# Cluster masks of the later head pairs moved from TensorE to VectorE, with first-layer weight sums and loads moved in the order

## The chip, the core and the metric

The kernel runs on one core of a Trainium2 chip. The metric is device time in microseconds (us) of the whole launch; less is better. A timed run has no profiler attached; one further execution was recorded by the hardware profiler, and all views and durations below come from it.

## The reference

Routed attention followed by a two-layer network with a hard-swish gate, everything in float32:

```python
# q, k, v: (4, 8, 768, 64), centroids: (8, 16, 64), w_in: (512, 2048), w_out: (2048, 512)
q_assign = argmax(normalised(q) . normalised(centroids))     # one of 16 clusters for each query
k_assign = argmax(normalised(k) . normalised(centroids))     # and for each key
mask = q_assign[:, :, :, None] == k_assign[:, :, None, :]
scores = where(mask, q @ k^T / 8, -1e9)
attn = softmax(scores);  x = attn @ v                        # a query sees the keys of its own cluster
# x as (3072, 512) tokens
h = x @ w_in;  g = h * clip(h + 3, 0, 6) / 6;  out = g @ w_out
```

## The kernel before

Attention works on *pairs* of heads, `g` = 0 to 15 (four batches of four pairs). A pair has 12 *items* `n`: two halves of the queries (`hf`, 384 each) times six chunks of 128 keys (`j`). For one item, both heads at once (64 rows of the array each):

- `scores` (line 419) writes keys by queries into PSUM: one f32 part from `xf` (q and k turned by `turn`) and one bf16 part from `xm`. `xm` holds the one-hot cluster vectors, turned by `route_turn` (line 367); on the side of k they hold -2^60 in every cluster but the key's own. The sum of the two parts is the score where the clusters agree and about -2^60 where they don't, so the exponential is 0 there. That is the mask.
- `exponentials` (line 434, ScalarE) writes `ex`; there are six buffers of it.
- `key_sums` (lines 454 and 457, GpSimd) adds `ex` up over the chunks, into `acc`.
- `attn_v` (line 467, TensorE) adds `ex` times v into `pv`; after six chunks `divide` sums `acc` over partitions by TensorE (`pd`, line 488), takes the reciprocal on VectorE (492), and multiplies (493). The result goes to DRAM as `xd`.

Before a pair can start, it is loaded (`load`, line 195, six DMAs on SyncE's queue), turned (310), routed (`cluster_scores` 323, `route` 334 to 343: scores against the centroids, maximum, one-hot) and its one-hots are turned (367).

The network works on 12 *blocks* of 256 tokens. A block is 8 *up* items and 7 *down* items. Both layers use a scheme with fewer multiplications (Strassen's, in Winograd's form), so sums of weights are needed. For the first layer these are `tx` (T1, T2, T4 of one up item; line 570), made once, written to DRAM as `td` and loaded again for the later blocks (line 573), two items ahead, into three buffers; T3 overwrites a part of `w_in_sb`. The up items of block 0 use plain products (603). An up item of the later blocks (`halved`) writes two PSUM banks, `uX` and `uY` (line 648; one of each, in turn), which VectorE reads with six sums and copies (659, 666); then ScalarE lifts (516), VectorE clips (519), and after every second item GpSimd makes four sums (`gated_sums`, 638). A down item (683) is one 128x256x1024 product, with the sums of y on VectorE (690).

The order of all engines is written out by hand (`tc.manual_schedule()`): each engine runs its instructions in the order in which the loop below emits them. The loop over `n` takes two items at a time (a *step*; `r` is the step's place in the pair, 0, 2, ... 10). From `DECODED` (item 96, pair 8) on, `four_by_four` runs: steps with r = 2, 6 and 10 emit scores and exponentials, and then a *fill* of four or five network items, with the preparation of the next pair between them (turns at r = 2, routing at 6, one-hots at 10); steps with r = 0, 4 and 8 emit scores, exponentials, the division and `attn_v` of four items, and key sums. `later` and `checks` hold work for the step after (the store of `num`, range checks).

`MASKED` is the first pair whose masks VectorE makes; before, it is `NPAIR` (16), so that none are, and `by_vector`, `clusters`, `spread` and `masks` are never in effect.

Of the kernel before, what the change touches and what calls it, by code (L numbers as in the profile page):

```python
# [17 lines left out]
C = 16  # L18
# [98 lines left out]
def fast_path(ctx, tc, ok, q, k, v, centroids, moe_w_in, moe_w_out, out):  # L117
# [48 lines left out]
    counts = const.tile([P, 2, NPAIR], F32, name="counts")  # L166
    w_low = const.tile([P, 1], F32, name="w_low")

    MASKED = NPAIR
    st = {}  # L170
    later = []
    numbers = []
# [87 lines left out]
    cen = startp.tile([P, D], F32, name="cen")  # L260
    parity = const.tile([P, 2], F32, name="parity")

    number = const.tile([P, C], BF16, name="number")

    def constants():
        make_identity(nc, ident)
        for t in range(2):
            nc.vector.tensor_reduce(
                out=parity[:, t : t + 1],
                in_=ident.rearrange("p (h t c) -> p t h c", t=2, c=C)[:, t], axis=AX.XY, op=ALU.max,  # L270
            )
        nc.gpsimd.memset(half_c, 0.5)
        nc.gpsimd.memset(low_c, 1.0 / BOUND)
        nc.gpsimd.memset(ones, 1.0)
        nc.gpsimd.memset(w_low, W_LOW)
        nc.gpsimd.memset(one_hot, 0.0)
        for c in range(C):
            nc.gpsimd.memset(number[:, c : c + 1], float(c))

        warm = psum_t.tile([P, 4, P], F32, name="warm", tag="t")  # L280
        for i in range(14):
            nc.tensor.transpose(out=warm[:, i % 4], in_=ident, identity=ident)
# [47 lines left out]
    def route(g):  # L330
        cs = st.pop(("cs", g))
        pr = scratch([P, NC2, 2, C], "pr")
        for i in range(NC2 // 4):
            nc.tensor.transpose(out=pr[:, 4 * i : 4 * i + 4], in_=cs[:, i], identity=ident)
        pr = pr.rearrange("p j t c -> p (j t) c")
        mx = rtp.tile([P, 2 * NC2], F32, name="mx")
        nc.vector.reduce_max(out=mx, in_=pr, axis=AX.X)
        oh = one_hot.rearrange("p j (t c) -> p j t c", t=2)[:, :, :, 0:C]
        pr = pr.rearrange("p (j t) c -> p j t c", t=2)
        mx = mx.rearrange("p (j t) -> p j t", t=2)  # L340
        halves = [slice(0, NCH), slice(NCH, NC2)]
# [14 lines left out]

        later.append(count)
        if g >= MASKED:
            numbers.append(lambda: clusters(g))

    def route_turn(g, part):
        if part == 0:
# [11 lines left out]
        return where(n)[0] >= MASKED  # L374

    def clusters(g):
        oh = one_hot.rearrange("p j (t c) -> p j t c", t=2)[:, :, :, 0:C]
        which = rtp.tile([P, NC2, 2, C], BF16, name="which")
        nc.vector.tensor_tensor(
            out=which, in0=oh, in1=number.unsqueeze(1).unsqueeze(1).to_broadcast([P, NC2, 2, C]), op=ALU.mult  # L380
        )
        qid = st["qid"] = rtp.tile([P, NCH, 2], BF16, name="qid")
        kid = st["kid", g] = kidp.tile([P, NCH, 2], F32, name="kid")
        nc.vector.tensor_reduce(out=kid, in_=which[:, NCH:], axis=AX.X, op=ALU.add)

        nc.vector.tensor_scalar(
            out=kid, in0=kid, scalar1=-1.0, scalar2=C * (C - 1) / 2.0, op0=ALU.mult, op1=ALU.add
        )
        qsum = rtp.tile([P, NCH, 2], F32, name="qsum")
        nc.vector.tensor_reduce(out=qsum, in_=which[:, 0:NCH], axis=AX.X, op=ALU.add)  # L390
        nc.vector.tensor_copy(out=qid, in_=qsum)

    def spread(g, part):
        if part == 0:
# [13 lines left out]
        return (g, *divmod(r, NCH))  # L408

    def scores_qk(n):  # L410
        g, hf, j = where(n)
        st["ps", n] = psum_s.tile([P, 2, 512], F32, name="ps")
        scores_part(n, st["xf", g], True)

    def scores_part(n, x, first):
        g, hf, j = where(n)
        for t in range(2):
            r = slice(t * D, (t + 1) * D)
            nc.tensor.matmul(  # L419
                st["ps", n][:, t, 0:HALF], lhsT=x[r, NCH + j],  # L420
                rhs=x[r, hf * NHC : (hf + 1) * NHC], start=first,
                stop=not first or by_vector(n),
            )

    def scores(n):
        if ("ps", n) not in st:
            scores_qk(n)
        if not by_vector(n):
            scores_part(n, st["xm", where(n)[0]], False)

    def exponentials(n):
        sc = st.pop(("ps", n))[:, :, 0:HALF]
        ex = st["ex", n] = expp.tile([P, 2, HALF], F32, name="ex")
        nc.scalar.activation(out=ex, in_=sc, func=ACT.Exp, scale=SM_SCALE)  # L434

# [12 lines left out]

# [111 lines left out]
    def first_sums(u):  # L560

        blk, i = divmod(u, HF)
        if not 0 < blk < B * NHC:
            return
        tx = st["tx", u] = txp.tile([P, 3, HK, P], F32, name="tx")
        if blk == 1:
            t1, t2, t4 = (tx[:, k] for k in range(3))
            b11, b12, b21, b22 = wi(0, 0, i), wi(0, 1, i), wi(1, 0, i), wi(1, 1, i)
            for out_, in0, in1 in ((t1, b12, b11), (t2, b22, t1), (t4, b21, t2), (b12, b22, b12)):
                nc.vector.tensor_tensor(out=out_, in0=in0, in1=in1, op=ALU.subtract)  # L570
            nc.sync.dma_start(td[:, i], tx)
        else:
            nc.sync.dma_start(tx, td[:, i])

    def token_sums(b, m):

# [15 lines left out]
    def ffn_items(b):  # L592
        def up(m, i):
            def item():
                load_block()
                u = (b * NHC + m) * HF + i
                g = g_sb[:, 0:4, i]
                if u < HF:
                    ph = psum_m.tile([P, 512], F32, name="ph", tag="m")
                    for t in range(2):  # L600
                        f = t * HF + i
                        for kt in range(NKT):
                            nc.tensor.matmul(  # L603
                                ph[:, t * HC : (t + 1) * HC], lhsT=w_in_sb[:, kt, f * P : (f + 1) * P],
                                rhs=st["xb", b, m][:, kt], start=(kt == 0), stop=(kt == NKT - 1),
                            )
                    ph = ph.rearrange("p (k c) -> p k c", k=4)
                    lift(g, ph)
                    clip(g, g, ph)
                    gated_sums(i)  # L610
                else:
                    halved(b, m, u, i, g)
                if u >= HF or i < HF - 2:
                    first_sums(u + 2)
                if i == HF - 1:
                    st.pop(("xb", b, m)), st.pop(("xs", b, m), None)
                    st["free"] = True
                    load_block()
                    finish()

            return item
# [70 lines left out]
        def down(m, part):  # L692
            def item():
# [85 lines left out]

    st["early"] = st["free"] = True  # L780
    st["last"] = False
    fill, checks, unmasked = [], [], []
    st["done"], st["valued"] = 0, DECODED - lag_v

    def check_all():
# [8 lines left out]
    def four_by_four(n, r, steps):  # L794
        for i in steps:
            scores(i)
        if r % 4 == 2:
# [22 lines left out]
        for i in range(st["valued"], min(n, total)):  # L820
            attn_v(i)
            if i % per_pair == NCH - 1:
                later.append(divide(i))
        st["valued"] = min(n, total)
        for i in steps[1 if r == 8 else 2 :]:
            exponentials(i)
        for i in steps:
            masks(i)
            key_sums(i)

    with tc.manual_schedule():
# [18 lines left out]
        for n in range(0, total + lag_d + 2, 2):  # L850
# [436 lines left out]
```

## Time and profile before

| | us |
|---|---|
| median of three timed runs | 1033.52 (1029.15 to 1035.98) |
| the profiled execution | 1026.24 |
| its span, first to last instruction | 1024.4 |
| TensorE (PE) busy | 997.8 (97%) |
| VectorE (DVE) busy | 562.8 (55%) |
| ScalarE (ACT) busy | 390.0 (38%) |
| GpSimd (POOL) busy | 433.3 (42%) |
| granted TensorE clock | 0.997 of full speed |

The chain that ended last is followed back from the last instruction; its shares tell who holds up the end. Busy shares are means over stages that differ: until about 250 us the weights are decoded beside the attention and all engines are busy; from there to 797 us attention and network alternate; the rest is network alone. A busy TensorE is not one at its peak, and the ends of its rows are modelled, so starts are compared. In a row of the timeline the first number is the start in us from the start of the span, the second the length; what stands in brackets is the idle time of that engine just before, and what ended it. A row can merge several instructions (xN).

### The profile page before, as it was taken

What the parts mean: (1) busy time and instruction counts of PE and PEld (TensorE: products, weight loads), DVE (VectorE), ACT (ScalarE), POOL (GpSimd) and SP (SyncE); (2) the same over time, 40 slices, a digit from 0 to 9 for tenths busy, and PEclk for the clock granted to TensorE, in tenths of its full rate; (3) what the DMA queues carried; (4) which work ended last, traced back from release to release, by engine and by line L of the source; (5) the groups of instructions that cost most, each with busy time, mean ns of one, the idle gap of its engine ahead of it and who ended that gap; (6) DMA issues with size and microseconds to landing.
All of it is one profiled execution on the core that took longest, in us unless ns stands there. A gap on an engine that the chain in (4) does not pass through costs nothing.

```text
span 1024.4 us, 16727 instructions
## 1 busy us (share of the span) xinstructions
PE 997.8 (97%) x6560; PEld 738.4 (72%) x6560; DVE 562.8 (55%) x1085; ACT 390.0 (38%) x764; POOL 433.3 (42%) x363
## 2 busy tenths in 40 slices
PE   8999999999999999999999999999999999999996
PEld 4444445546778777778787777678787898999995
DVE  4899977868368245226336236227246272727270
ACT  6888876675233233233323333333223020202010
POOL 4777756766325426426415415524516230303030
PEclk9999999999999999999999999999999999999999
DMA  6355664532223222223224025023023051414120
GB/s 177 101 145 144 165 165 97 143 86 46 58 91 110 55 91 83 54 75 103 58 83 118 27 68 152 9 70 98 29 84 97 3 154 40 143 40 126 51 63 25
DMA packets 107176, 90.34 MB, mean 88 GB/s; under 512 B 78416, under 2 KB 88656, under 8 KB 107088
## 3 DMA queue, kind: packets, MB, share of 16 engines
q1 hardware_dynamic: 106944, 89.15, 31.1%
q8 instruction: 54, 0.88, 0.3%
q14 instruction: 34, 0.28, 0.1%
q10 hardware_dynamic: 144, 0.03, 0.0%
HBM read 73.43 MB, written 15.73 MB: 87 GB/s over the span
## 4 chain that ended last, share of the span: by engine, by line
PE 84%; ACT 4%; DVE 4%; DMA 4%; SPq 2%; issue 1%; POOL 0%; ACTq 0%; DVEq 0%; POOLq 0%
PE Y L683 16%; PE uY L648 14%; PE ps L419 12%; PE X L683 12%; PE uX L648 11%; PE pv L467 9%; PE ph L603 3%; SPq L195 2%; PE pd L488 2%; PE pqk L310 2%; DMA raw<-in_moe_w_in_dram 1%; ACT ex L434 1%; PE pcs L323 1%; DMA tx<-td 1%; DVE wunit L247 1%
## 5 line engine op out<-in xcount | busy, mean ns | idle before, releaser
L457 POOL TENSOR_TENSOR acc<-acc,ex 128x768 f32<-128x768 f32 x128 | 241.3, 1885 | 139.0 <-ACT ex L434 132.6
L638 POOL TENSOR_TENSOR g_sb<-g_sb 128x256 f32<-128x256 f32 x176 | 130.5, 763 | 325.9 <-DVE g_sb L519 322.5
L434 ACT ACTIVATE ex<-ps 128x768 f32<-128x768 f32 x192 | 148.4, 806 | 87.4 <-PE ps L419 75.3
L516 ACT ACTIVATE sx<-g_sb,half_c 128x512 f32<-128x512 f32 x88 | 63.5, 722 | 277.5 <-DVE g_sb L659 277.5
L419 PE MATMUL ps<-xf 64*128 64x384 f32 x768 | 165.5, 509 | 2.7 <-ACT ex L434 2.6
L467 PE MATMUL pv<-ex,vt 128*64 128x384 f32 x768 | 141.1, 496 | 0.0
L690 DVE TENSOR_TENSOR y<-y,Y 128x256 f32<-128x256 f32 x48 | 20.2, 421 | 175.5 <-PE Y L683 174.7
L467 PEld LDWEIGHTS pv<-ex,vt 128*64 128x64 f32 x768 | 48.7, 136 | 78.2 <-issue 70.0
L492 DVE RECIPROCAL rcp<-pd 128x384 f32<-128x384 f32 x32 | 81.8, 2556 | 41.4 <-PE pd L488 41.3
L419 PEld LDWEIGHTS ps<-xf 64*128 64x128 f32 x768 | 63.1, 186 | 53.1 <-issue 36.5
L454 POOL TENSOR_TENSOR acc<-ex 128x768 f32<-128x768 f32 x32 | 59.8, 1867 | 94.9 <-ACT ex L434 94.9
L648 PE MATMUL uX<-xb,w_in_sb 128*128 128x128 f32 x704 | 93.8, 277 | 0.0
L683 PE MATMUL X<-w_out_sb,g_sb 128*128 128x256 f32 x384 | 89.7, 381 | 0.0
L683 PE MATMUL Y<-T,g_sb 128*128 128x256 f32 x384 | 87.3, 380 | 0.0
L683 PE MATMUL Y<-w_out_sb,g_sb 128*128 128x256 f32 x384 | 87.2, 380 | 0.0
L648 PEld LDWEIGHTS uX<-xb,w_in_sb 128*128 128x128 f32 x704 | 86.5, 194 | 0.0
L683 PEld LDWEIGHTS X<-w_out_sb,g_sb 128*128 128x128 f32 x384 | 71.3, 190 | 12.6 <-issue 3.8
L683 PEld LDWEIGHTS Y<-T,g_sb 128*128 128x128 f32 x384 | 72.3, 190 | 11.1 <-issue 1.6
L683 PEld LDWEIGHTS Y<-w_out_sb,g_sb 128*128 128x128 f32 x384 | 72.2, 190 | 11.0 <-issue 1.6
L519 DVE SCALAR_TENSOR_TENSOR g_sb<-sx,g_sb 128x512 f32<-128x512 f32 x88 | 66.9, 764 | 1.0 <-ACT sx L516 0.9
L419 PE MATMUL ps<-xm 64*128 64x384 bf16 x384 | 63.1, 323 | 3.1 <-ACT xm L369 2.8
L659 DVE TENSOR_TENSOR g_sb<-uY,sx 128x128 f32<-128x128 f32 (+1 forms) x176 | 65.7, 414 | 0.1
(110 smaller groups left out, 1381.5 us busy)
## 6 DMA issues: line engine op xcount, KB each, us to landing
tx<-td SPq DMA_DIRECT2D x80, 384.0 KB, 3.2
raw<-in_moe_w_in_dram SPq DMA_DIRECT2D x16, 512.0 KB, 3.8
raw<-in_moe_w_out_dram SPq DMA_DIRECT2D x16, 512.0 KB, 3.7
qk<-in_q_dram SPq DMA_DIRECT2D x32, 192.0 KB, 4.3
qk<-in_k_dram SPq DMA_DIRECT2D x32, 192.0 KB, 4.6
vt<-in_v_dram SPq DMA_DIRECT2D x32, 192.0 KB, 4.2
xd<-num SPq DMA_DIRECT2D x32, 192.0 KB, 2.4
xb<-xd SPq DMA_DIRECT2D x12, 512.0 KB, 4.0
```

What stands on the lines that cost most here:

```text
L419: nc.tensor.matmul(st["ps", n][:, t, 0:HALF], lhsT=x[r, NCH + j], rhs=x[r, hf * NHC : (hf + 1) * NHC], start=first, stop=not first or by_v ...
L434: nc.scalar.activation(out=ex, in_=sc, func=ACT.Exp, scale=SM_SCALE)
L454: nc.gpsimd.tensor_tensor(out=acc, in0=st["ex", n - 1], in1=ex, op=ALU.add)
L457: nc.gpsimd.tensor_tensor(out=acc, in0=acc, in1=ex, op=ALU.add)
L467: nc.tensor.matmul(pv[t * D : (t + 1) * D], lhsT=vt[:, j, t], rhs=ex[:, t], start=(j == 0), stop=(j == NCH - 1),)
L492: nc.vector.reciprocal(out=rcp, in_=pd)
L516: nc.scalar.activation(out=r, in_=h, func=ACT.Relu, bias=half_c, scale=1.0 / 6.0)
L519: nc.vector.scalar_tensor_tensor(out=g, in0=r, scalar=1.0, in1=h, op0=ALU.min, op1=ALU.mult)
L638: eng.tensor_tensor(out=out_, in0=in0, in1=in1, op=op)
L648: nc.tensor.matmul(dst, lhsT=w[:, kt], rhs=x(kt), start=(kt == 0), stop=(kt == HK - 1))
L659: nc.vector.tensor_tensor(out=out_, in0=in0, in1=in1, op=ALU.add)
L683: nc.tensor.matmul(bank[:, half * HC : (half + 1) * HC], lhsT=g_sb[:, kind, i], rhs=w[:, i], start=(first and i == 0), stop=(last and i == ...
```

## The change

1. `MASKED` becomes 9. For pairs 9 to 15 `scores` emits the f32 part alone. `clusters` turns the one-hots into cluster numbers (VectorE; two products, one reduction, one copy), `spread` writes each query's number onto all partitions (12 bf16 matmuls and three copies by ScalarE, in the place of `route_turn`), and `masks` multiplies `ex` in place by (query's number == key's number), one VectorE instruction for each head of an item.
2. Where the masks stand on VectorE: for steps with r = 2, 6 and 10 they are queued as `singles` and emitted one behind each fill item, except behind the first at r = 6, where the routing is; for the other steps at the step's end, but at r = 8 those of the step's first item stand before the division.
3. In the other pairs, the bf16 part of the scores is emitted in front of the f32 part, except at a pair's first item.
4. All first-layer weight sums are made beside the seven down items of block 0 (`make_first_sums`); block 1 loads them as the later blocks do, but for two that are kept.
5. From pair 8 on, the loads of the step with r = 6 are emitted behind the fill instead of in front of it.

```diff
-    MASKED = NPAIR
+    MASKED = NPAIR // 2 + 1
...
-    number = const.tile([P, C], BF16, name="number")
+    number = const.tile([P, 2, C], BF16, name="number")
...
-            nc.gpsimd.memset(number[:, c : c + 1], float(c))
+            nc.gpsimd.memset(number[:, 0, c : c + 1], c - C * (C - 1) / 2.0)
+            nc.gpsimd.memset(number[:, 1, c : c + 1], -float(c))
...
         if g >= MASKED:
-            numbers.append(lambda: clusters(g))
+            numbers.extend(clusters(g))
...
     def clusters(g):
...
+        oh = one_hot.rearrange("p (h j) (t c) -> p h j t c", h=2, t=2)[:, :, :, :, 0:C]
+        which = rtp.tile([P, 2, NCH, 2, C], BF16, name="which")
         qid = st["qid"] = rtp.tile([P, NCH, 2], BF16, name="qid")
+        kid = st["kid", g] = kidp.tile([P, 2, NCH, 2], F32, name="kid")
+        def weigh():
+            for h in range(2):
+                nc.vector.tensor_tensor(
+                    out=which[:, h], in0=oh[:, h],
+                    in1=number[:, h].unsqueeze(1).unsqueeze(1).to_broadcast([P, NCH, 2, C]), op=ALU.mult,
+                )
+        def collect():
+            nc.vector.tensor_reduce(out=kid, in_=which, axis=AX.X, op=ALU.add)
+        def narrow():
+            nc.vector.tensor_copy(out=qid, in_=kid[:, 0])
+        return [weigh, collect, narrow]
...
     def scores(n):
+        g, hf, j = where(n)
         if ("ps", n) not in st:
-            scores_qk(n)
+            if hf == j == 0 or by_vector(n):
+                scores_qk(n)
+            else:
+                st["ps", n] = psum_s.tile([P, 2, 512], F32, name="ps")
+                scores_part(n, st["xm", g], True, False)
+                scores_part(n, st["xf", g], False, True)
+                return
         if not by_vector(n):
-            scores_part(n, st["xm", where(n)[0]], False)
+            scores_part(n, st["xm", g], False, True)
...
-    def masks(n):
+    def masks(n, heads=(0, 1)):
...
         ex = st["ex", n]
-        for t in range(2):
+        for t in heads:
             nc.vector.scalar_tensor_tensor(
                 out=ex[:, t].rearrange("p (a b) -> p a b", b=P),
                 in0=st["xm", g][:, t * NCH + hf * NHC : t * NCH + (hf + 1) * NHC],
-                scalar=st["kid", g][:, j, t : t + 1], in1=ex[:, t].rearrange("p (a b) -> p a b", b=P),
+                scalar=st["kid", g][:, 1, j, t : t + 1], in1=ex[:, t].rearrange("p (a b) -> p a b", b=P),
                 op0=ALU.is_equal, op1=ALU.mult,
             )
...
     def first_sums(u):
         blk, i = divmod(u, HF)
-        if not 0 < blk < B * NHC:
-            return
-        tx = st["tx", u] = txp.tile([P, 3, HK, P], F32, name="tx")
-        if blk == 1:
...
-            nc.sync.dma_start(td[:, i], tx)
-        else:
+        if ("tx", u) not in st and 0 < blk < B * NHC:
+            tx = st["tx", u] = txp.tile([P, 3, HK, P], F32, name="tx")
             nc.sync.dma_start(tx, td[:, i])
+    def make_first_sums(i):
+        tx = txp.tile([P, 3, HK, P], F32, name="tx")
+        t1, t2, t4 = (tx[:, k] for k in range(3))
+        b11, b12, b21, b22 = wi(0, 0, i), wi(0, 1, i), wi(1, 0, i), wi(1, 1, i)
+        for out_, in0, in1 in ((t1, b12, b11), (t2, b22, t1), (t4, b21, t2), (b12, b22, b12)):
+            nc.vector.tensor_tensor(out=out_, in0=in0, in1=in1, op=ALU.subtract)
+        nc.sync.dma_start(td[:, i], tx)
+        if i < 2:
+            st["tx", HF + i] = tx
...
-                if u >= HF or i < HF - 2:
+                if u >= HF:
                     first_sums(u + 2)
...
-                if (b, m) == (0, 0) and part > 4:
-                    first_sums(HF + part - 5)
+                if (b, m) == (0, 0):
+                    for i in ([HF - 1, HF - 2], [5], [4], [3], [2], [0], [1])[part]:
+                        make_first_sums(i)
...
             unmasked.extend(steps)
             check_all()
-            for op in numbers:
-                op()
-            numbers.clear()
+            for i in steps:
+                singles.extend(lambda i=i, t=t: masks(i, [t]) for t in range(2))
             return
...
         for i in unmasked:
-            masks(i)
             key_sums(i)
...
             attn_v(i)
             if i % per_pair == NCH - 1:
+                for k in steps[:1]:
+                    masks(k)
                 later.append(divide(i))
...
         for i in steps:
-            masks(i)
+            if r != 8 or i != steps[0]:
+                masks(i)
             key_sums(i)
...
-            if r == 6:
+            if r == 6 and not fours:
                 load(g + 2, "q", "k")
                 load(g + 1, "v")
...
                     if i < want:
                         fill.pop(0)()
+                    if singles and (r != 6 or i > 0):
+                        singles.pop(0)()
                     if i < len(prep):
                         prep[i]()
+                if fours:
+                    for op in singles + numbers:
+                        op()
+                    singles.clear(), numbers.clear()
+            if r == 6 and fours:
+                load(g + 2, "q", "k")
+                load(g + 1, "v")
```

More of the change, by code (lines that the diff above doesn't have):

```diff
@@ L376, in clusters @@
     def clusters(g):
[L377 to L381, printed above, removed]
-        qid = st["qid"] = rtp.tile([P, NCH, 2], BF16, name="qid")
[L383 to L391, printed above, removed]
+        oh = one_hot.rearrange("p (h j) (t c) -> p h j t c", h=2, t=2)[:, :, :, :, 0:C]
+        which = rtp.tile([P, 2, NCH, 2, C], BF16, name="which")
+        qid = st["qid"] = rtp.tile([P, NCH, 2], BF16, name="qid")
+        kid = st["kid", g] = kidp.tile([P, 2, NCH, 2], F32, name="kid")
[10 more added lines that the diff above has]
+        return [weigh, collect, narrow]
     def spread(g, part):
@@ L410, in scores_qk, with scores_part @@
     def scores_qk(n):
-        g, hf, j = where(n)
         st["ps", n] = psum_s.tile([P, 2, 512], F32, name="ps")
-        scores_part(n, st["xf", g], True)
-    def scores_part(n, x, first):
+        scores_part(n, st["xf", where(n)[0]], True, by_vector(n))
+    def scores_part(n, x, first, last):
         g, hf, j = where(n)
@@ L420, in scores_part @@
                 st["ps", n][:, t, 0:HALF], lhsT=x[r, NCH + j],
-                rhs=x[r, hf * NHC : (hf + 1) * NHC], start=first,
-                stop=not first or by_vector(n),
+                rhs=x[r, hf * NHC : (hf + 1) * NHC], start=first, stop=last,
             )
     def scores(n):
+        g, hf, j = where(n)
         if ("ps", n) not in st:
-            scores_qk(n)
+            if hf == j == 0 or by_vector(n):
[5 more added lines that the diff above has]
+                return
         if not by_vector(n):
-            scores_part(n, st["xm", where(n)[0]], False)
+            scores_part(n, st["xm", g], False, True)
     def exponentials(n):
@@ L562, in first_sums @@
         blk, i = divmod(u, HF)
-        if not 0 < blk < B * NHC:
-            return
-        tx = st["tx", u] = txp.tile([P, 3, HK, P], F32, name="tx")
-        if blk == 1:
[L567 to L570, printed above, removed]
-            nc.sync.dma_start(td[:, i], tx)
-        else:
-            nc.sync.dma_start(tx, td[:, i])
+        if ("tx", u) not in st and 0 < blk < B * NHC:
+            tx = st["tx", u] = txp.tile([P, 3, HK, P], F32, name="tx")
+            nc.sync.dma_start(tx, td[:, i])
+    def make_first_sums(i):
[7 more added lines that the diff above has]
+            st["tx", HF + i] = tx
     def token_sums(b, m):
@@ L781, in fast_path @@
     st["last"] = False
-    fill, checks, unmasked = [], [], []
+    fill, checks, unmasked, singles = [], [], [], []
     st["done"], st["valued"] = 0, DECODED - lag_v
```

## The prediction

> **What bounds the kernel now.** I read the chain that ended last first, then the busy time by stage, then the instructions in order of time where the change works.
>
> ```profile
> PE 84%; ACT 4%; DVE 4%; DMA 4%; SPq 2%; issue 1%; POOL 0%; ACTq 0%; DVEq 0%; POOLq 0%
> ```
>
> TensorE carries 84% of the chain; nobody else has more than 4%. The stage that matters begins with pair 9 (the tenth) and ends with the last attention item. The first scores of pair 9 start at 316 us and the last attention work is over at 797 us.
>
> ```profile
> core 0: us, PE busy (x) PEld busy (x) DVE busy (x) ACT busy (x) POOL busy (x), PEclk, DMA share, GB/s
> ...
> 316.00:797.00 481.00, 477.00 (x3216) 365.69 (x3215) 214.17 (x467) 155.16 (x278) 206.57 (x178) 1.00 0.27 77
> ```
>
> The columns are the length, then busy time and instruction count of PE, PE's weight loads, DVE, ACT and POOL. In these 481 us TensorE is idle for 4.0 us, VectorE is busy for 214 us (45%) and GpSimd for 207 us (43%). So in this stage TensorE time taken away shortens the run, and work given to VectorE is free only as long as it comes in time for TensorE.
>
> **Gain 1: the mask matmuls.** TensorE's rows for one step of two items:
>
> ```profile
> 342.48 0.92 PE L419 MATMUL ps<-xf 64*128 64x384 f32 x4
> 343.23 0.33 PE L419 MATMUL ps<-xm 64*128 64x384 bf16 x2
> 343.39 0.81 PE L419 MATMUL ps<-xf 64*128 64x384 f32 x4
> 344.04 0.33 PE L419 MATMUL ps<-xm 64*128 64x384 bf16 x2
> 344.30 0.85 PE L323 MATMUL pcs<-xf,cnT 128*32 128x384 f32 x8
> ```
>
> The end of a row is modelled, so starts are compared. The mask part begins at 343.23 and the next scores at 343.39: 0.16 us; the two heads run beside each other. The second one begins at 344.04 and the next kind of work at 344.30: 0.26 us, of which 0.10 is the change of kind, since every step from these matmuls to another shape shows 0.09 to 0.10 and the plain scores would pay it too. So an item loses 0.16 us. Pairs 9 to 15 have 7 x 12 = 84 items: **13.7 us** with the 0.163 that the starts give on average. What replaces the one-hot transposes costs TensorE nothing more: 12 bf16 matmuls of 128x128 a pair before (6 and 6, 56 ns from start to start) and 12 of that size after (4, 4 and 4). ScalarE copies 3 x 0.59 us for 2 x 0.81, and it is busy for a third of the stage.
>
> In the other pairs the mask part now goes in front of the scores part, except at a pair's first item. The same instructions stand in another order and the 0.10 us for a change of shape is paid at both ends either way. Bounds: 0.1 us gained or lost in each of some 50 steps, 5 us either way; I take 0, because both kinds use the same 64-row shape.
>
> **Gain 2: the weight sums T1, T2, T4 of the first layer (now line 570).** Before, most of these sums stand on VectorE behind the up items of block 1; TensorE then waits for VectorE:
>
> ```profile
> 301.76 0.28 DVE L666 COPY sx<-uX 128x128 f32<-128x128 f32 x1
> ...
> 302.75 0.71 PE L648 MATMUL uX<-xs,tx 128*128 128x128 f32 x4 [0.23 <-DVE sx L659]
> ...
> 304.52 1.70 DVE L570 TENSOR_TENSOR tx<-w_in_sb,tx 128x256 f32<-128x256 f32 x2
> 306.15 0.94 DVE L570 TENSOR_TENSOR w_in_sb<-w_in_sb 128x256 f32<-128x256 f32 x1
> 307.01 0.28 DVE L666 COPY sx<-uX 128x128 f32<-128x128 f32 x1
> ...
> 307.99 1.03 PE L648 MATMUL uX<-xs,tx 128*128 128x128 f32 x4 [1.85 <-DVE sx L659]
> ```
>
> At 301.76 VectorE comes 1.4 us after the end of its matmuls and TensorE waits 0.2 us; at 307.01 it comes 2.6 us after and TensorE waits 1.85 us. (These two also give the allowance that I use below: VectorE may be **about 1.2 us late** before TensorE stands, because the next item's uX only needs the bank of the last one.) The stretch from 307 to 312 us has a granted clock of 0.66, and the item from 307.99 to 312.84 takes 4.85 us instead of 3.14, 1.7 us more. Sum: 0.4 + 2.0 + 1.7 = **4.1 us**. After, the sums stand beside the down items of block 0, 8 x 1.7 us in 24 us of matmuls that ask VectorE for 4 us of other sums; I cost that at nothing. If GpSimd's key sums block them (see below) they take up to 9 us more; a down item's y sum then comes 4 us later and its bank is wanted 7 us later. Block 1 loads its sums as later blocks do: one tx load an item, two items (6.3 us) ahead, against a landing time of 3.2 us (median). Bounds 2 to 5 us.
>
> **Gain 3: loads behind the fill in the step with r = 6.** On SyncE's queue:
>
> ```profile
> 548.89 1.24 SPq L195 DMA_DIRECT2D qk<-in_q_dram  x2
> 550.18 1.33 SPq L195 DMA_DIRECT2D qk<-in_k_dram  x2
> 551.56 2.57 SPq L195 DMA_DIRECT2D vt<-in_v_dram  x2
> 554.23 1.94 SPq L573 DMA_DIRECT2D tx<-td  x3
> 558.57 0.68 PE L648 MATMUL uX<-xs,tx 128*128 128x128 f32 x4 [2.31 <-DMA tx<-td]
> ```
>
> Six loads are issued between 548.89 and 554.13, and the tx loads for the up items stand behind them: TensorE waits 2.31 us here and 1.44 at 627 us, the only two such waits. After, the loads follow the tx loads of their fill group and have until the next group, one attention step of 6 us later, which covers the 5.3 us of issuing; q, k and v are wanted in the next pair. Gain **3.8 us**, bounds 2 to 4.
>
> **Cost: 168 masks on VectorE.** No row shows this operation: scalar_tensor_tensor, 128x384, bf16 and f32 in, f32 out, both tensors in SBUF. The nearest is line 493, 128x384 with two f32 tensors in SBUF, and it has two prices:
>
> ```profile
> 294.85 0.56 DVE L493 TENSOR_TENSOR num<-num,rcp 128x384 f32<-128x384 f32 x1
> ...
> 546.24 7.69 POOL L457 TENSOR_TENSOR acc<-acc,ex 128x768 f32<-128x768 f32 x4
> 546.95 1.51 DVE L493 TENSOR_TENSOR num<-num,rcp 128x384 f32<-128x384 f32 x1
> ```
>
> Alone it takes 0.56 us; beside GpSimd's key sums 1.51. The key sums run from 546.24 at 1.82 us each; VectorE's operation, due at 546.95, can start only when the first of them ends at 548.05. The Trainium skill ("SBUF — State Buffer", section "Who interferes with whom") says the same and says it against this change: a VectorE instruction with two SBUF inputs and a GpSimd instruction that reads SBUF exclude each other, and the later one blocks for the whole of the other. By that rule with every mask meeting a key sum: mean wait 0.91 + 0.56 = 1.47 us, 247 us in all, and VectorE would have 214 + 247 = 461 us of work in a stage of 463 us. By the rows GpSimd is busy for 43% of the stage: 0.56 + 0.43 x 0.91 = **0.95 us**, 160 us in all. With 9 us for the cluster numbers (per pair two products 0.2, a reduction 0.55, a copy 0.2, some waiting) and 6 us of first-layer sums gone, VectorE has 377 us: 81%. I take 0.95; ends 0.56 and 1.5.
>
> What then reaches TensorE is lateness in front of up items, since a down item needs no VectorE result for two parts. An up item asks 2.66 us of VectorE in 3.14 us of TensorE; with a mask behind it 3.2 (alone) to 4.1.
> - After r = 0: the four masks of a step (0.56 each, and two waits for a key sum) are done about when the next uX ends. No wait.
> - After r = 4, counted from the step's first score: scores to 1.36, pd to 2.2, then the reciprocal until 4.9 and the product until 5.5; two masks to 6.6; the third waits for the key sum of the first item (1.82) and ends at 8.95, the fourth at 9.5. On TensorE: pv to 5.0, scores to 6.4, pcs to 7.2, uX to 8.6. VectorE is 0.7 us late, inside the allowance (before it was idle for 2.6 us there). The routing then adds 1.17 us in front of the second item, which wants VectorE at 12.5 and gets it at 13.65: 0.4 us of waiting. The third, behind the first single mask and perhaps four gated sums of 0.73, waits 0 to 1.1. About 0.9 us a group, in the four groups (pairs 11 to 14) that begin with up items and hold a routing: 3.6.
> - After r = 8 one step's masks stand in front of the reciprocal, which waits for pd behind two pv anyway (3.6 us); the cluster numbers (1.3) stand ahead. Late by 0.8 to 1.8: three groups begin with an up item (pairs 9, 14, 15), 0.6 each: 1.8.
> - The masked exponentials reach pv and the key sums later. pv of the last item is wanted 3.4 us after the step's first score, its mask is done at 2.25. GpSimd has 57% idle time. The eleven other groups with up items: 0.1 each.
>
> Sum: **6.5 us**, between 2 (masks mostly alone) and 20 (1.2 us a mask: two steps with 4.4 up items then ask VectorE for 4.4 x 2.66 + 8 x 1.2 = 21 us in TensorE's 21). The skill ("TensorE: Matmul & The Clock Gate", section "What's actually happening") would let a short stand be free of a clock loss: half rate follows an idle window of some 3.4 us. The trace disagrees in one case of three: the 1.85 us wait was followed by the slow stretch above, those of 2.31 and 1.44 were not. My waits stay near 1 us, so I add nothing; if they reached 2 us, a third of them would cost 1.7 more.
>
> **Sum.** 13.7 + 4.1 + 3.8 - 6.5 = 15 us. Against the profiled execution (1026.24 us, span 1024.4) that is 1011; the three timed runs have a median of 1033.52, 7 us above it, so on their scale **1018.5 us**, faster by 1.5%.
>
> **Rivals.**
> 1. **VectorE is always in time.** For it: 55% idle in the stage, and the masks are spread one behind an item. Against it: the two-price row. Gain 21.6 minus 1: 1013.
> 2. **The waits eat most of it.** Same mechanism as my cost at its upper end, with masks at 1.2 us: 18 us of waits, 3.6 us left: 1030, no change. For it: an up item leaves VectorE only 0.5 us. Against: 7 of 15 items are down items, where it recovers.
> 3. **VectorE becomes the bound, slower.** Place: the pairs 9 to 15; price: each mask above 1.46 us, where 217 (214 + 9 - 6) + 168 x 1.46 reaches TensorE's 463 us; at 1.7 us (each mask waits for a whole key sum, as the third does in the step with r = 4) VectorE needs 503 us, 22 more than the stage has now; with gain 2 back, 1051. For it: a key sum is released by just these masks, so it starts between them. Against: of four masks in a row only one or two can meet one, and the singles meet none or a gated sum of 0.73.
> 4. **The loads or the sums only move.** tx waits reappear elsewhere and block 0 is delayed: 8 us less, 1026.5.
>
> **Chances.** Forecast 55%, rival 1 15%, rival 2 15%, rival 3 7%, rival 4 8%. A measurement of this kernel tells about 1% (10.3 us) from no change; faster by over 1% means below 1023.2. That is nearly all of the forecast's and rival 1's cases: 70%; within 1%: 22%, from rivals 2 and 4 and the forecast's upper edge; slower by over 1%: 8%. The range from 1007 to 1031 holds rivals 1, 2 and 4, and leaves out rival 3 and a timed median that lies as low as the profiled run.
>
> **What would show it.** Right: no mask part on TensorE between 316 us and the end of attention, mask rows of 0.8 to 1.1 us on average (0.56 alone), VectorE near 80% in that stage and TensorE's idle time there under 10 us; no wait for tx; no wait for VectorE in block 1 and no clock of 0.66 there. Wrong: mask rows above 1.4 us, TensorE waiting over 15 us for VectorE's copies of uX, or ScalarE's exponentials waiting for the key sums.

## The result, and the profile after

| | before | after |
|---|---|---|
| median of the timed runs, first comparison | 1033.33 us | 1021.33 us |
| ratio, with its 95% interval | | 0.9895 (0.9856 to 0.9933) |
| ratio in a second comparison, on the chip of other experiments | | 0.993 (0.9905 to 0.9955) |
| span of the profiled execution | 1024.4 us | 1022.6 us |

The change makes the kernel faster by 1.05% (12 us) in the first comparison and by 0.7% in the second, where 1.5% (15 us) was forecast. The two profiled executions lie only 1.8 us apart. Their first part can't be compared from one execution each: from the first `attn_v` of all to that of pair 8, executions of kernels with the very same instructions there (after and its variants) took between 251.0 and 256.5 us. So later stages are compared, not spans. They are cut at TensorE's `pv` rows: the first of pair 8, the first of pair 9, the last of all. (The first six items of pair 9 lie before the second cut, so the last stage holds 78 of the 84 masked items.)

The two stages in after's profile (length; busy time and count of PE, weight loads, DVE, ACT, POOL; granted clock; DMA share; GB/s):

```profile
273.95:339.38 65.43, 65.43 (x458) 51.00 (x456) 45.31 (x95) 22.98 (x44) 29.25 (x26) 1.00 0.40 114
339.38:793.51 454.13, 442.82 (x2900) 341.08 (x2896) 329.04 (x622) 144.37 (x270) 199.16 (x162) 1.00 0.28 76
```

The same cuts in before's profile:

```profile
268.82:339.80 70.98, 68.81 (x469) 53.33 (x467) 47.89 (x102) 23.16 (x43) 30.92 (x27) 0.98 0.30 93
339.80:795.68 455.88, 451.96 (x3055) 347.37 (x3052) 199.29 (x438) 145.89 (x264) 187.64 (x162) 1.00 0.27 76
```

Pair 8, where the first-layer sums no longer stand beside the up items, is 5.5 us shorter, TensorE is never idle in it and the granted clock is full. The **masked stage**, which gives up 156 of its matmuls on TensorE, is shorter by only 1.75 us: TensorE's idle time went from 3.9 to 11.3 us, and VectorE is busy for 329 us of 454 (72%) instead of 199. What TensorE waited for there, after first, then before (in all, times, longest):

```profile
PE uX L664 <- DVE sx L675: 8.2, 10, 2.4
PE X L699 <- DVE sx L675: 2.1, 1, 2.1
PE pb L405 <- DVE rcp L505: 0.5, 1, 0.5
PE pv L480 <- ACT num L486: 0.3, 2, 0.2
```

```profile
PE uX L648 <- DMA tx<-td: 3.8, 2, 2.3
PE uX L648 <- DVE sx L659: 0.2, 1, 0.2
```

The two waits for tx are gone, and waits for VectorE's reading of uX have taken their place. The masks themselves, from after's costliest groups (count | busy us, mean ns of one | idle before):

```profile
L455 DVE SCALAR_TENSOR_TENSOR ex<-xm,kid,ex 128x384 f32<-128x384 bf16 x168 | 132.8, 825 | 10.0 <-ACT ex L447 10.0
```

Their median is 610 ns and their longest 2179; 29 of the 168 are longer than 0.7 us, and each of these meets an operation of GpSimd.

To see what the stage gained and lost, TensorE's time from start to start is summed by what the matmul writes, over the masked stage of three kernels (e1, below, is after without masks on VectorE):

| us in the masked stage | before | e1 | after |
|---|---|---|---|
| ps (scores) | 70.8 | 67.6 | 58.1 |
| pr (routing), with the wait behind it | 2.0 | 2.0 | 9.4 |
| uY, with the wait behind it | 91.7 | 88.9 | 91.1 |
| X and Y | 143.8 | 143.8 | 144.8 |
| pv, uX, pd, po or pb | 136.4 | 136.6 | 139.4 |
| the others (pcs, pqk) | 11.2 | 11.3 | 11.2 |
| stage | 455.9 | 450.1 | 454.1 |

Against e1 the masks save 9.5 us of scores in this stage and cost 13.5 us elsewhere: 4.0 us are lost. Pair 9's six items before the cut give 0.8 us back in pair 8 (66.19 us in e1, 65.43 in after). So **moving the masks loses 3.2 us**, and what makes after faster than before is the rest of the change.

### The profile page after: what moved, and what is told of

It is laid out like the page before. It is cut to its first block, busy times and chain, and to the rows that moved or that the text cites. A ratio compares the mean times of both kernels' runs of the same rounds, so it can differ in the third digit from the quotient of the medians.

```text
span 1022.6 us, 16587 instructions
## 1 busy us (share of the span) xinstructions
PE 983.8 (96%) x6392; PEld 731.5 (72%) x6392; DVE 708.5 (69%) x1281; ACT 388.5 (38%) x771; POOL 444.4 (43%) x379
## 5 line engine op out<-in xcount | busy, mean ns | idle before, releaser
L470 POOL TENSOR_TENSOR acc<-acc,ex 128x768 f32<-128x768 f32 x128 | 244.0, 1906 | 180.7 <-DVE ex L455 89.9
L654 POOL TENSOR_TENSOR g_sb<-g_sb 128x256 f32<-128x256 f32 x176 | 137.9, 805 | 279.5 <-DVE g_sb L532 268.4
L447 ACT ACTIVATE ex<-ps 128x768 f32<-128x768 f32 x192 | 146.1, 805 | 77.4 <-PE ps L424 74.7
L424 PE MATMUL ps<-xf 64*128 64x384 f32 x768 | 154.0, 496 | 0.9 <-ACT ex L447 0.9
L455 DVE SCALAR_TENSOR_TENSOR ex<-xm,kid,ex 128x384 f32<-128x384 bf16 x168 | 132.8, 825 | 10.0 <-ACT ex L447 10.0
L424 PEld LDWEIGHTS ps<-xf 64*128 64x128 f32 x768 | 67.1, 187 | 38.8 <-issue 23.8
L699 PEld LDWEIGHTS Y<-T,g_sb 128*128 128x128 f32 x384 | 72.2, 190 | 11.2 <-issue 1.7
L532 DVE SCALAR_TENSOR_TENSOR g_sb<-sx,g_sb 128x512 f32<-128x512 f32 x88 | 70.5, 807 | 0.0
```

The costliest lines, as they stand in the source:

```text
L424: nc.tensor.matmul(st["ps", n][:, t, 0:HALF], lhsT=x[r, NCH + j], rhs=x[r, hf * NHC : (hf + 1) * NHC], start=first, stop=last,)
L455: nc.vector.scalar_tensor_tensor(out=ex[:, t].rearrange("p (a b) -> p a b", b=P), in0=st["xm", g][:, t * NCH + hf * NHC : t * NCH + (hf + ...
L470: nc.gpsimd.tensor_tensor(out=acc, in0=acc, in1=ex, op=ALU.add)
L532: nc.vector.scalar_tensor_tensor(out=g, in0=r, scalar=1.0, in1=h, op0=ALU.min, op1=ALU.mult)
L654: eng.tensor_tensor(out=out_, in0=in0, in1=in1, op=op)
L699: nc.tensor.matmul(bank[:, half * HC : (half + 1) * HC], lhsT=g_sb[:, kind, i], rhs=w[:, i], start=(first and i == 0), stop=(last and i == ...
```

## The experiments

Ratios are timed, each against runs of before on the same chip; e5, e6, e7 and e10 share a chip, and so do e1 to e4, on which after was not timed. "Stage" is the masked stage in the profile, and is steadier: two profiles of after gave 454.13 and 454.12.

| | what | ratio (interval) | pair 8 | stage |
|---|---|---|---|---|
| before | | 1 | 70.98 | 455.88 |
| after, e5 | twice | 0.9895, 0.993 | 65.43 | 454.13 |
| e1 | no masks on VectorE | 0.9881 (0.9863 to 0.9900) | 66.19 | 450.13 |
| e2 | f32 part first again | 0.9950 (0.9929 to 0.9971) | 65.71 | 454.12 |
| e3 | sums in block 1 again | 0.9963 (0.9949 to 0.9977) | 69.57 | 455.78 |
| e4 | loads first again | 0.9934 (0.9917 to 0.9951) | 65.43 | 455.57 |
| e6 | before, bf16 part first | 0.9958 (0.9942 to 0.9974) | 69.47 | 454.79 |
| e7 | r = 4: two masks later | 1.0001 (0.9980 to 1.0021) | 65.43 | 466.64 |
| e10 | key sums left out | 0.9843 (0.9808 to 0.9879) | 65.43 | 444.58 |
| e9 | e1, copy on ScalarE | 0.9865 (0.9835 to 0.9896) | 66.30 | 449.52 |
| e11 | after, copy on ScalarE | 0.9905 (0.9872 to 0.9938) | 65.44 | 452.40 |
| e12 | masks in pairs 9, 10 only | 0.9861 (0.9829 to 0.9893) | 65.43 | 448.99 |
| e13 | e12, copy on ScalarE | 0.9840 (0.9810 to 0.9869) | 65.44 | 447.85 |

**e1: no masks on VectorE.**

```diff
-    MASKED = NPAIR // 2 + 1
+    MASKED = NPAIR
```

> MASKED is 16 again: no mask moves to VectorE, the rest of the change stays. Theory (the profile of after): the masks give 13.6 us of TensorE time and take about 12 back in waits of TensorE for VectorE at the first up items behind the steps with r = 4, so this kernel is within 3 us of after, 9 to 12 us faster than before, and in its profile no wait of TensorE for VectorE over 1 us stands between pair 9 and the end of attention. Rival (the prediction's own sum, 13.7 - 6.5): the masks are worth 7 us, so this kernel is 7 us slower than after.

The theory holds, and more than it said: timed, e1 is no slower than after (0.9881 against 0.9895 and 0.993), and pair 8 and the stage together are 3.2 us shorter. TensorE waits for VectorE 1.1 us there in all, never over 0.5 at a time.

```profile
PE uX L664 <- DVE sx L675: 1.1, 3, 0.5
```

**e2: the old order of the two score parts.** In `scores`, the branch that emits the bf16 part first is taken out:

```diff
-            if hf == j == 0 or by_vector(n):
-                scores_qk(n)
-            else:
...
-                scores_part(n, st["xm", g], True, False)
-                scores_part(n, st["xf", g], False, True)
-                return
+            scores_qk(n)
```

> After with the f32 part of the scores in front of the bf16 part in pairs 0 to 8, as before. Theory: the order is worth nothing, within 2 us of after, and the first 270 us of the profiles differ by no more than two executions of one kernel. Rival: it is the order that made the first 156 us of after's profile 5 to 6 us longer than before's; then this kernel is 5 us faster than after. Second rival: the order is worth the 5 us upper bound of the prediction; then it is 5 us slower than after.

Timed, e2's ratio is 0.995, that of after 0.9895 and 0.993: 2 to 6 us slower, with overlapping intervals, which speaks for the second rival but doesn't settle it. The order touches pairs 0 to 8 alone here, where the lengths of profiles scatter. e6 was made for that.

**e6: the order alone, in all pairs of the kernel before.** The branch that e2 takes out, put into before's `scores`.

> The kernel before with nothing but the order of the two score parts changed (bf16 part in front, except at a pair's first item), in all 16 pairs. Theory: worth nothing, within 2 us of before. Rival: e2's time against the others' means it is worth about 5 us; then this kernel is 4 to 6 us faster than before, and the gain stands in the pairs before pair 8 as well as behind.

The rival holds: 0.9958, 4.3 us faster than before (2.7 to 6.0). Where it comes from can be read in the rows of one step with the bf16 part in front, from after's pair 8:

```profile
298.40 0.34 PE L424 MATMUL ps<-xm 64*128 64x384 bf16 x2
298.57 0.81 PE L424 MATMUL ps<-xf 64*128 64x384 f32 x4
299.22 0.33 PE L424 MATMUL ps<-xm 64*128 64x384 bf16 x2
299.38 0.81 PE L424 MATMUL ps<-xf 64*128 64x384 f32 x4
```

From start to start the parts are 0.17, 0.65, 0.16. In before's step, shown with the prediction, they are 0.75, 0.16, 0.65: the first f32 part behind another shape of work takes 0.10 us more than the second one. With a bf16 part in front it doesn't. The score rows of before and e1 say the same: 70.8 less 67.6 us over 39 steps is 0.08 a step. It is there in the early pairs too: up to pair 8's first `attn_v`, 50 steps take 94.0 us of score rows in before and e2, and 90.2 in after and e6.

In e6's stage only 1.1 of the 3.2 us show. One wait for tx became longer, 2.9 us, and from its end on the granted clock is low (0.50 for 3.4 us in all); the rows of uX and uY, with their waits, take 2.0 us more than in before.

```profile
PE uX L653 <- DMA tx<-td: 4.4, 2, 2.9
```

In all of e6 the score rows save 7.5 us (95 steps). Less these 2.0, 5.5 are left in this execution; the timed runs show 4.3 of them.

**e3: the sums beside block 1 again.** `first_sums` makes the sums of block 1 (two of them in the last two down items of block 0), and the list of `make_first_sums` in `down` goes.

> After with the first-layer weight sums beside the up items of block 1 again. Theory: it loses the 5.5 us that the stretch from pair 8 to pair 9 gained in the profile (65.4 against 71.0 us), and the clock under 1 comes back there: 4 to 7 us slower than after. Rival: other work fills the same waits, within 2 us of after.

The theory holds in the amount: pair 8 takes 69.57 instead of 65.43 us, and TensorE waits there for VectorE again:

```profile
PE uX L665 <- DVE sx L676: 3.0, 4, 1.6
```

The low clock didn't come back in this pair: it was full, so a wait of 1.6 us needn't cost the clock. That e3's stage is 1.7 us longer than after's arises elsewhere: behind the wait of 2.1 us in pair 11, which after has too, the clock is 0.50 for 3.4 us here and full in after.

**e4: the loads in front of the fill again.**

```diff
-            if r == 6 and not fours:
+            if r == 6:
                 load(g + 2, "q", "k")
                 load(g + 1, "v")
...
-            if r == 6 and fours:
-                load(g + 2, "q", "k")
-                load(g + 1, "v")
```

> After with the loads of r = 6 in front of the fill again. Theory: waits for tx come back, two of 1.5 to 2.5 us as before: 3 to 4 us slower than after. Rival: TensorE already waits for VectorE at the same up items (r = 6), so the tx loads arrive within those waits and nothing is lost: within 1 us of after.

The rival holds. No wait for tx comes back, and TensorE's waits for VectorE are after's: 8.2 and 2.1 us. The stage is 1.4 us longer, but that arises in one up item of pair 13, behind a wait of 2.4 us that after has at the same place. The clock fell there in this execution; the same stretch in e4 and in after (the clock is the third number from the end):

```profile
617.50:620.90 3.40, 3.40 (x18) 3.40 (x17) 2.16 (x7) 0.24 (x1) 0.00 (x0) 0.50 0.58 219
622.15:625.55 3.40, 3.14 (x28) 2.95 (x27) 3.30 (x11) 0.47 (x2) 0.00 (x0) 1.00 0.20 46
```

So with the masks on VectorE the place of the loads is worth nothing that these runs show. Without masks it is worth more: uY, with the wait behind it, falls from 91.7 (before) to 88.9 us (e1).

**e5: after once more.**

> The changed kernel once more, on the chip of this call, so that the others can be set against it. Theory: 10 to 12 us faster than before, and its profile shows the same three stands of 2 to 2.7 us behind the routing of pairs 11 to 13, while the first 270 us differ by several us from the first profile of the same kernel (they hang on when weight chunks land).

The stage repeats to 0.01 us and the three stands come back at the same places (2.4, 2.7 and 2.7 us from pr to the next matmul); the early part differs by 1.6 us. Timed it is 0.993, 7 us faster than before, less than the 10 to 12 expected.

**e7: two masks of the step with r = 4 later.**

```diff
         for i in steps:
+            if r == 4 and i == steps[1]:
+                singles.extend(lambda i=i, t=t: masks(i, [t]) for t in range(2))
+                unmasked.append(i)
+                continue
             if r != 8 or i != steps[0]:
```

> After, but of the four masks of a step with r = 4 the two of the second item are queued behind the fill items of the step with r = 6 (its key sum follows them). Theory (VectorE comes late to the first up item because reciprocal, product and four masks with their waits for key sums stand in front of it): the three stands behind the routing fall from 2 to 2.7 us to under 1, so 4 to 6 us faster than after. Rival (VectorE's work in an all-up group is too much as a sum, so that a mask moved back only makes the wait appear at a later up item): within 1.5 us of after.

The three stands are gone, as the theory said: from pr to the next matmul it is 0.11 us in pairs 11, 12 and 13, as in e1, and pair 11 takes 65.4 instead of 67.8 us. With two masks in front of it instead of four, VectorE's copy of uX in pair 11 is in time, and TensorE goes on:

```profile
475.63 2.71 DVE L455 SCALAR_TENSOR_TENSOR ex<-xm,kid,ex 128x384 f32<-128x384 bf16 x2
478.26 0.28 DVE L682 COPY sx<-uX 128x128 f32<-128x128 f32 x1
...
479.57 1.89 PE L699 MATMUL X<-w_out_sb,g_sb 128*128 128x256 f32 x8
```

The gain fails to come all the same: the stage is 12.5 us longer. The item moved is the last of a half, and its key sum is wanted by pd in the step with r = 8. The key sum now follows its masks, and pd waits:

```profile
PE pd L501 <- POOL acc L470: 9.3, 4, 5.2
PE uX L664 <- DVE sx L675: 5.5, 6, 2.2
```

Of the 12.5 us TensorE is idle for 4.4 more than in after; for the other 8.2 it is busy longer with the same 2900 matmuls. Four stretches of this stage have half the clock, each behind a wait of about 2 us or more; this is the longest, from 636 us, in which the wait of 5.2 us ends.

```profile
636.00:643.00 7.00, 6.06 (x20) 2.43 (x20) 6.91 (x6) 0.26 (x1) 4.46 (x3) 0.51 0.20 34
```

So masks can't simply be put behind the fill; the key sums have a due time of their own.

**e10: without most key sums.**

```diff
-        elif j > 1:
+        elif j > 1 and g < MASKED:
```

> After, with the key sums left out from the third chunk on in the masked pairs (the denominators are then sums over two chunks only). Theory (a mask's length above 0.61 us and most of TensorE's waiting come from the exclusion of GpSimd's key sums and VectorE's two-input operations): mask rows average under 0.68 instead of 0.825 us, product rows (506) 0.56, TensorE's waits for VectorE between pair 9 and the end of attention fall from about 15 us to under 7, and the kernel is 6 to 10 us faster than after. Rival (the amount of VectorE work itself): waits fall by less than 3 us.

The theory holds. (The kernel's denominators are incomplete; it is a measurement only.) Masks are 661 ns on average (825 in after), the products of the stage's 14 divisions 567 ns (886 in after), TensorE's waits for uX's reading fall from 8.2 to 2.6 us, and the stage is 9.5 us shorter than after's, 5.5 shorter than e1's. Timed, the ratio is 0.9843 against 0.9895 and 0.993. Only 10 masks are longer than 0.7 us, and the three stands are gone here too (0.11 us).

```profile
L455 DVE SCALAR_TENSOR_TENSOR ex<-xm,kid,ex 128x384 f32<-128x384 bf16 x168 | 105.0, 661 | 11.3 <-ACT ex L447 11.3
PE uX L664 <- DVE sx L675: 2.6, 7, 1.1
```

So about 9.5 of the 13.5 us that the masks cost hang on GpSimd's key sums. (Without key sums pd can't wait for them either, but after's pd waits for none, as its list above shows.) The other 4 us were not isolated.

**e9 and e11: the copy of uX on ScalarE**, without and with the masks.

```diff
-            nc.vector.tensor_copy(out=sx[:, 1], in_=X[:, 1])
+            nc.scalar.copy(out=sx[:, 1], in_=X[:, 1])
```

> The kernel of e1 (no masks by VectorE) with the first copy of each up item (uX to sx, line 682) on ScalarE instead of VectorE. Theory: TensorE waits for VectorE only twice by 0.7 us in e1, so relief of VectorE is worth nothing: within 2 us of e1, that is 10 to 14 us faster than before. Rival: the hop to ScalarE and back lengthens the chain of every up item: 3 us slower than e1 or more.

> After, with the same copy on ScalarE. Theory: VectorE's backlog in front of the up items falls by 0.3 us an item and the copy no longer stands behind masks, so the three stands behind the routing shrink by 0.5 to 1.5 us each and the stage from pair 9 to the end of attention is 450 to 453 us instead of 454.1; 1 to 4 us faster than after. Rival: the sums that follow the copy are late all the same, since they are VectorE's: stage 453.5 to 455.

e9's theory holds: its stage is 449.5 (e1: 450.1), and the copy takes 261 ns on ScalarE (292 on VectorE). e11's stage is 452.4, 1.7 us shorter than after's, as its theory had it; but each of the three stands shrinks by no more than 0.3 us, not 0.5 to 1.5, which is the rival's point: the sums behind the copy are VectorE's and late with it. Timed, 0.9905 is no clear gain over after.

**e12 and e13: masks only in the pairs whose routing stands beside down items.**

```diff
-    MASKED = NPAIR // 2 + 1
+    VECTOR = (9, 10)
...
-        return where(n)[0] >= MASKED
+        return where(n)[0] in VECTOR
```

(and the same in `route` and `prep_items`; e13 has the copy on ScalarE too.)

> After with masks by VectorE in pairs 9 and 10 alone; the others are masked by TensorE. Theory: in these two pairs the fill behind the routing begins with down items, which need nothing from VectorE, and after gained 2.1 us there against e1 (65.5 and 68.5 us against 66.2 and 70.0): the stage is 447 to 449 us, against 450.1 in e1 and 454.1 in after. Rival: the gain of a masked pair without routing behind an up item is eaten by later waits: 450 or more.

> e12 and the copy on ScalarE together. Theory: no more than e12 (stage 446 to 449 us); the fastest of all by a little, 11 to 15 us faster than before. Rival: the copy costs what it costs in e9.

e12's stage is 449.0, 1.1 us under e1, and with pair 8 it is 1.9 us: by the profiles the masks pay in these two pairs, though the timed intervals of e12 and e1 overlap. e13 is the fastest complete kernel by its timed ratio, 1014.25 us against 1030.76 of before on that chip (0.984). Its advantage over e12 and e9 lies within the intervals. Its stage:

```profile
338.28:786.13 447.85, 447.49 (x3019) 345.11 (x3016) 219.11 (x434) 154.57 (x313) 191.47 (x163) 1.00 0.29 77
```

TensorE is idle for 0.4 us in 448.

## Why the prediction was right, and where its sum was off

The direction was right and 1021.3 lies in the range; the size was forecast as 15 us and came out as 12 and 7. That the sum came so near is luck in part. In the stage where the masks move, the forecast amounts to 12.7 + 3.8 - 6.5 = 10 us for its 78 items, and 1.75 came. Pair 8 gave 5.5, and the order of the score parts, put at 0, took 3.8 us from the score rows of the earlier pairs. By its steps:

- **Gain 1, the mask matmuls: right.** 13.7 us for 84 items were forecast; the score rows of the stage, which has 78 of them, show 70.8 - 58.1 = 12.7, which is 0.163 an item. But 3.2 of these come from the new order alone, without a mask on VectorE (e1); against the better order the masks are worth 9.5.
- **Gain 2, the first-layer sums: right.** 4.1 forecast; 4.1 in e3 against after. In pair 8 of before against after it is 5.5, of which 0.8 belong to the first masked items of pair 9. The clock's part of 1.7 was in before's profile and not in e3's, where the waits are longer (3.0 us); that both make 4.1 is chance. Costing the sums at nothing beside block 0 was right: TensorE waits for nothing in after's pair 8.
- **Gain 3, the loads: over-sized beside the masks.** 3.8 forecast, nothing in e4, whose 1.4 us are the clock's. The two waits for tx went, but TensorE now stands for VectorE at the up item just before, and the prediction didn't ask whether it would. Without masks they are worth 2.8 (uY's rows in e1).
- **The order of the score parts: mis-sized at 0.** The bound of 0.1 us a step was right and so was the cause of it, a change of shape. The choice of 0 assumed the loss to be the same at both ends; but the rows quoted in the prediction already had it once more, in 0.75 against 0.65 us for the first and second f32 part. Measured: 0.08 a step, and 4.3 us timed for all pairs (e6).
- **The cost: mis-sized, 6.5 forecast and 13.5 measured.** Not by the amounts: a mask averages 0.825 us (0.95 taken) and VectorE is busy for 72% of the stage (81%). The step that failed is the ledger of the step with r = 4. Here it is in after, pair 11, whose first score starts at 471.21:

```profile
473.62 2.56 DVE L505 RECIPROCAL rcp<-pd 128x384 f32<-128x384 f32 x1 [0.75 <-PE pd L501]
473.76 2.11 POOL L654 TENSOR_TENSOR g_sb<-g_sb 128x256 f32<-128x256 f32 x3
475.82 3.92 POOL L470 TENSOR_TENSOR acc<-acc,ex 128x768 f32<-128x768 f32 x2
476.21 1.84 DVE L506 TENSOR_TENSOR num<-num,rcp 128x384 f32<-128x384 f32 x1
477.98 5.32 DVE L455 SCALAR_TENSOR_TENSOR ex<-xm,kid,ex 128x384 f32<-128x384 bf16 x4
...
480.86 2.03 POOL L470 TENSOR_TENSOR acc<-acc,ex 128x768 f32<-128x768 f32 x1 [1.12 <-DVE ex L455]
...
483.22 0.28 DVE L682 COPY sx<-uX 128x128 f32<-128x128 f32 x1
...
484.20 1.99 PE L699 MATMUL X<-w_out_sb,g_sb 128*128 128x256 f32 x8 [2.13 <-DVE sx L675]
```

The forecast let the product (0.56) and two masks find GpSimd free, and put one wait for a key sum behind them, in front of the third mask. But key sums of earlier items are still due, and the gated sums of the last up items stand in front of them on GpSimd, until 4.6 us after the first score. The two key sums run from 475.82 to 479.74, just when VectorE has its product and its first mask to do: the product takes 1.84 us, and of the four masks the first and the last take 2.2 and the two between them 0.6. The copy of uX, due at about 480.0, comes at 483.22: 3.3 us late, where 0.7 was forecast. With the allowance of 1.2 that the prediction had read from the trace, a stand of 2.1 follows, which is the measured one. In e1, whose uX of this item starts within 0.05 us of after's, the same copy comes in time:

```profile
479.95 0.29 DVE L682 COPY sx<-uX 128x128 f32<-128x128 f32 x1 [2.41 <-PE uX L664]
```

Three such stands (pairs 11, 12 and 13) make 7.5 of the 13.5 us, as the growth of the pr rows shows; 0.9 each had been forecast. Two experiments show the cause: the stands go when two of the four masks stand elsewhere (e7), and they go when the key sums are left out (e10). The forecast's fourth group, in pair 14, shows no stand at that place: before its r = 4 the fill ends with three down items and one up item, so GpSimd has no gated sums there. The trace shows that step's product at 0.56 us, the four masks behind it at 3.76 together, and the copy of uX about 0.5 us late.

Weighing the Trainium skill's rule of exclusion ("SBUF — State Buffer", section "Who interferes with whom") against the rows was right in the mean: 29 of 168 masks lost 36 us in waiting for GpSimd, 0.22 a mask where 0.39 was taken. But a mean doesn't show that the waits fall together in front of the same item. Of the rivals, the second (the waits eat most of it) was the nearest for the masks alone, and after all went a step further: the masks lose. The third didn't come; VectorE isn't the bound. Of what the text named as signs, the masks' length, tx and block 1 came out right; VectorE's share is lower than the 80% named, and TensorE's idle time in the stage, 11.3 us, is over the 10 that were to stay unreached.

Left open: how much of the 3.8 us of score rows in pairs 0 to 7 reaches the end, since profiles of the same instructions differ there by 5 us; the 4 us of the masks' cost that don't hang on key sums; and how the two comparisons of after (0.9895 and 0.993, with intervals that overlap) divide between chips and runs.

## What to carry to other kernels

Work that is moved from the bound engine to an idle one is paid for where it comes late, not by its sum: write the receiving engine's order out for the worst step, with every engine that excludes it and what stands queued in front of that one, and move the work only in the steps where this order has room (pairs 9 and 10 here). When several edits are tried together, undo each alone: here three small ones made the gain and the large one in the title cost 3.2 us. Before a difference of stages is put down to an edit, look whether the clock was the same in both: all of e4's 1.4 us was a low clock behind a wait that both kernels had. Two rows of the same shape that differ in length (0.75 and 0.65) are a finding, not noise.

## What the runs showed of the hardware

- VectorE's masks and products (both tensors in SBUF) wait for the end of a whole GpSimd operation: 0.61 us alone, up to 2.18; two key sums in a row let one such operation through between them.
- The first f32 matmul part behind work of another shape takes 0.10 us longer than the next; a bf16 part of the same shape in front takes that away (0.75 against 0.65).
- The low clock comes at the end of waits of TensorE or just behind, but neither their length nor their place decides alone. Each stretch seen from pair 8 to the end of attention has a clock of 0.50 for 3.4 us (6.8 once, in e7). It came behind a wait of 1.85 us in before and of 2.4 and 5.2 in e7, not behind one of 2.3 in before. Behind the same wait of 2.1 us it came in e3 and not in after or e4, and behind the same 2.4 us in e4 and not in after or e3.
